# Attention and a two-layer mixer in one launch: when the third batch's q is loaded, and which queue turns it

## The chip, the cores and the metric

The kernel runs on one core of one Trainium2 chip. The metric is the device time of one execution in microseconds (us). The engines are named as in the profile: PE is TensorE (matmuls), PEld its weight loads, DVE is VectorE, ACT is ScalarE, POOL is GpSimd, SP is SyncE, which here only issues DMAs. A "q" behind an engine's name (SPq, ACTq) marks the DMA-issuing instructions of its queue. All transfers run on the core's 16 DMA engines, whoever issues them.

## The reference

All inputs are float32, and so is the output, of shape 8 × 384 × 1024.

```python
batch, n_q_heads, n_kv_heads, seq, head_dim = (8, 16, 4, 384, 64)
# attention: each of the 4 k/v heads serves 4 q heads
scores = scale * np.matmul(q, k.transpose(0, 1, 3, 2))
attn = softmax(scores)
x = np.matmul(attn, v)        # then heads side by side: (8, 384, 1024)
# mixer: over tokens, then over channels
tok = np.einsum('ts,bsd->btd', w_tok, alpha1 * x + beta1)
u = x + lam * tok
ch = np.maximum((alpha2 * u + beta2) @ w_ch1, 0.0) @ w_ch2    # 1024 -> 4096 -> 1024
out = u + lam * ch
```

## The kernel before

The work goes batch by batch, in eight **passes** (b = 0 to 7). A pass is what `main(b)` does: the two large products of batch b, with the attention and the token mixing of batch b + 1 (`side(b + 1)`) laid between its matmuls. Both matrices are bf16 on the chip.

**Phase 0 of a pass, "h"** (line 410): h = relu(a2 · W1). W1 (1024 × 4096) does not stay on the chip; it is read again in every pass, in 16 chunks of 256 columns (`load_w1`, 512 KB each as bf16), through a ring of five buffers (`RING`). GpSimd issues the load of chunk c + 5 as soon as chunk c's matmuls are done. Each chunk makes two 128-column tiles (`nt`) of 8 matmuls. ACT evacuates the even tiles and DVE the odd ones into `hT`. Two PSUM banks ("mm") take turns.

**Phase 1 of a pass, "ch"** (line 443): ch = h · W2, with W2 kept on the chip from the first pass on, in 2 × 3 output blocks of 32 matmuls each. Between every 4 matmuls there is room for a step of `side(b + 1)`: its scores (line 217, `scores3`), exp on ACT (line 226), attention times v (line 252), the token product (line 273) and a transposing DMA of the result into `a2T` (line 295), which is the next pass's h input.

**Slots.** `main` is a generator that yields 0 in phase 0 (twice per tile, 64 slots) and 1 in phase 1. The loop at the end of the kernel counts the yields of each phase and, at each count, calls what has been put down for that slot. The lists for `side` put the first `scores3` into slot 0 of phase 1. The list `moves` puts down loads and flips.

**q and k.** `load_k` reads k in float32 into `kst` (SP's queue), and `place_k` casts it into `k2` on GpSimd. `load_q` reads 16 heads of q in four loads of 4 heads each, with a cast to bf16, into the one buffer `q_raw` (GpSimd's queue, 192 KB each). `load_next(b)` does `place_k`, `load_q` and `load_v` in that order. The scores need q and k with the head dimension on partitions. For batches 0 and 1 PE transposes them. From batch 2 on a transposing DMA does: `flip_k` fills `kT` in one instruction, and `flip_q` fills `qT` in four, each for 4 heads (two of the eight pairs p). For batches 3 to 7 they are put into phase 1 of pass b − 2, at slots 34 to 43, on SP's queue, while that pass still works on the batch before; the scores of batch b follow in phase 1 of pass b − 1.

Batch 2 is the exception, since its loads come out of the busy start. Before the change its k and q are loaded at the end of phase 0 of pass 0, behind the first five W1 chunks of pass 1; the loads then wait their turn in GpSimd's DMA queue behind W2 and W1. They are flipped in phase 0 of pass 1, at slots 46 (k), 50, 54, 58 and 62 (q), from **ACT's** queue.

The order of instructions on every engine is the order in which the code records them (`manual_schedule`). Waits between engines are semaphores that the framework places. Each flip of q waits for the one load that fills its 4 heads.

Of the kernel before, what the change touches and what calls it, by code (L numbers as in the profile page):

```python
# [12 lines left out]
def kernel(  # L13
# [21 lines left out]
    nc = tc.nc  # L35
# [17 lines left out]
    NP = Hq // 2  # L53
    D1 = D + 1
    CW = 2
    NCH = NNT // CW
    RING = 5
# [21 lines left out]
    kT = const.tile([P, NST, Hkv, P], bf, tag="kT", name="kT")  # L79


    qT = const.tile([P, NP, NST, P], bf, tag="qT", name="qT")
# [3 lines left out]
    def by_st(ap):  # L86
        return ap.rearrange("h (p st) d -> p st h d", st=NST)
# [10 lines left out]
    def place_k(b, i, hs=(0, 1)):  # L98
        if b not in k2s:
            k2s[b] = sb.tile([P, NST, Hkv, 2, D], bf, tag="k2", name="k2", bufs=1)  # L100
        copies = [nc.gpsimd.tensor_copy] * 2
        if b == 1 or b == 0 == i:
            copies = (nc.vector.tensor_copy, nc.vector.tensor_copy if i else nc.scalar.copy)
        lo, hi = hs[0], hs[-1] + 1
        for a in range(2):
            copies[a](out=k2s[b][:, :, 2 * i + lo:2 * i + hi, a, :], in_=ks[b][i][:, lo:hi].rearrange("p h st d -> p st h d"))

    def load_v(b, sts=range(NST)):
        for st in sts:
            nc.gpsimd.dma_start(out=vt[b % 2][:, st, :, :D], in_=by_st(v[b])[:, st])  # L110

    def load_q(b):
        qrs[b] = sb.tile([P, Hq, NST, D], bf, tag="q_raw", name="q_raw", bufs=1)
        for h in range(0, Hq, G):
            nc.gpsimd.dma_start(out=qrs[b][:, h:h + G], in_=q[b, h:h + G].rearrange("h (p st) d -> p h st d", st=NST))

    def flip_queue(b):
        return nc.scalar if b == 2 else nc.sync

    def flip_k(b):  # L120
        flip_queue(b).dma_start_transpose(out=kT.rearrange("p st h s -> p (st h) s"),
                                    in_=k2s[b].rearrange("p st h a d -> p (st h a d)"))

    def flip_q(b, i=0, n=NP):
        flip_queue(b).dma_start_transpose(out=qT[:, i:i + n].rearrange("p a j s -> p (a j) s"),
                                    in_=qrs[b][:, 2 * i:2 * (i + n)].rearrange("p h st d -> p (h st d)"))

    w1src = moe_w_ch1.rearrange("(dt di) nf -> di dt nf", di=P)
# [3 lines left out]
    def load_w1(n):  # L132
        if n < B * NCH:
            t = sb.tile([P, NDT, CW * P], bf, tag="w1", name="w1", bufs=RING)
            c = n % NCH
            nc.gpsimd.dma_start(out=t, in_=w1src[:, :, c * CW * P:(c + 1) * CW * P])  # L136
            w1_tiles[n] = t

    def load_w2(dw, i, n):
        r, cs = slice(i * NNT // n, (i + 1) * NNT // n), slice(dw * 512, (dw + 1) * 512)  # L140
        nc.gpsimd.dma_start(out=w2[:, r, cs], in_=w2src[:, r, cs])

    def bank(shape, tag, name, dtype=f32):
        if tag == "mm":
            return mms.tile(shape, dtype, tag="mm", name=name, bufs=2)
        return psum.tile(shape, dtype, tag=tag, name=name, bufs=2 if tag == "sc" else 1)
# [9 lines left out]
    def evac(eng):  # L156
        return nc.scalar.copy if eng == "ACT" else nc.vector.tensor_copy
# [234 lines left out]
    def load_next(b):  # L392
        place_k(b, 0)
        place_k(b, 1)
        load_q(b)
        load_v(b)


    def main(b):
        a2T = a2Ts[b % 2]  # L400
        x = xs.pop(b)
        n = S + 1 if b == 0 else S
        for c in range(NCH):
            w1 = w1_tiles.pop(b * NCH + c)
            for j in range(CW):
                nt = c * CW + j
                begun = b == 0 and nt in early
                ps = early[nt] if begun else bank([P, 512], "mm", "h")
                for dt in range(0 if begun else NDT):
                    nc.tensor.matmul(out=ps[:, :n], lhsT=w1[:, dt, j * P:(j + 1) * P],  # L410
                                     rhs=a2T[:, dt, :n], start=(dt == 0), stop=(dt == NDT - 1))
                    if dt == 3:
                        yield 0
                c1 = bias1[:, nt:nt + 1]
                if b == 0:
                    evac("DVE" if nt % 2 else "ACT")(out=c1, in_=ps[:, S:n])
                if nt % 2 == 0:
                    nc.scalar.activation(out=hT[:, nt, :], in_=ps[:, :S], func=RELU, bias=c1)  # L418
                else:
                    nc.vector.tensor_scalar(out=hT[:, nt, :], in0=ps[:, :S], scalar1=c1,  # L420
                                            scalar2=0.0, op0=ADD, op1=mybir.AluOpType.max)
                yield 0

            if b or c + RING < NCH:
                load_w1(b * NCH + c + RING)
            if b == 0 and c == NCH - RING:
                for i in range(3, 8):
                    load_w2(0, i, 8)
                for i in range(8):
                    load_w2(1, i, 8)  # L430
            if b == 0 and c == NCH - 1:
                for i in range(RING):
                    load_w1(NCH + i)
                load_next(2)
        for dw in range(NDW):
            cs = slice(dw * 512, (dw + 1) * 512)
            for ms in range(NST):
                ps = bank([P, 512], "mm", "ch")
                o = sb.tile([P, 512], f32, tag="tmp", name="o", bufs=4)
                last = (b, dw, ms) == (B - 1, NDW - 1, NST - 1)  # L440
                for lo, hi in ((0, 256), (256, 384), (384, 512)) if last else ((0, 512),):
                    for nt in range(NNT):
                        nc.tensor.matmul(out=ps[:, lo:hi], lhsT=hT[:, nt, ms * P:(ms + 1) * P],  # L443
                                         rhs=w2[:, nt, dw * 512 + lo:dw * 512 + hi], start=(nt == 0), stop=(nt == NNT - 1))
                        if nt % 4 == 3 and nt < NNT - 1:
                            yield 1
                    c = slice(dw * 512 + lo, dw * 512 + hi)
                    nc.vector.tensor_tensor(out=o[:, lo:hi], in0=ps[:, lo:hi], in1=lam_t[:, c], op=MUL)  # L448
                    nc.vector.tensor_tensor(out=o[:, lo:hi], in0=o[:, lo:hi], in1=x[:, ms, c], op=ADD)  # L449
                    nc.sync.dma_start(out=out[b].rearrange("(p st) d -> p st d", st=NST)[:, ms, c], in_=o[:, lo:hi])  # L450
                yield 1
# [3 lines left out]
    with tc.manual_schedule(engines=order):  # L455
# [103 lines left out]
        for b in range(B):  # L559
            us = side(b + 1) if b + 1 < B else ({}, {})  # L560


            moves = []
            if b == 1:
                moves = [(0, 46 + 4 * i, flip_q, 2, 2 * i - 2, 2) if i else (0, 46, flip_k, 2) for i in range(5)]
            if 0 < b < B - 2:
                moves += [(1, 1, load_k, b + 2), (1, 2, load_next, b + 2), (1, 34, flip_k, b + 2), (1, 36, flip_q, b + 2, 0, 2),
                          (1, 37, flip_q, b + 2, 2, 2), (1, 42, flip_q, b + 2, 4, 2), (1, 43, flip_q, b + 2, 6, 2)]
            for i, u, *m in moves:
                us[i].setdefault(u, []).append(m)  # L570
            done = [0, 0]
            for second in main(b):
                if b == second - done[1] - 1 == 0:
                    lead_banks.close()
                    threes.append(ST(tc.psum_pool(name="threes", bufs=3)))
                for f, *a in us[second].get(done[second], []):
                    f(*a)
                done[second] += 1
# [28 lines left out]
```

The softmax here doesn't subtract the row's maximum and nothing guards it: scores larger than these inputs give would overflow.

## Time and profile before

| | |
|---|---|
| time, median of 3 | 806.16 us (805.33 to 807.13) |
| profiled span | 803.5 us |
| PE busy | 793.8 us (99%), 6123 matmuls |
| ACT busy | 226.9 us (28%) |
| DVE busy | 343.5 us (43%) |
| POOL busy | 178.5 us (22%) |
| moved by DMA | 113.17 MB, mean 141 GB/s |

A busy share tells how full an engine is over the whole span; where the kernel waits is read from the stages. The second pass, which the change touches, runs from 133.44 us (its first h matmul) to 232.50 us (the next pass's first). Its phase 1 begins at 176.75 us. In the profile's groups, `w` is a chunk of W1 or a part of W2, `sc` a bank of scores, `es` their exp, and `a<-b` reads "a is written from b". In the timeline a line gives start, duration, engine, source line, instruction, and in brackets how long the engine was idle before it and who ended that.

### The profile page before, as it was taken

The numbers are of one execution on the slowest core, as the hardware profiler recorded it, in microseconds if no ns is written. First come the engines' busy times: TensorE is split into PE (matmuls) and PEld (weight loads), VectorE is DVE, ScalarE is ACT, GpSimd is POOL, SyncE is SP. The second block draws the span as 40 slices with busy tenths as digits, with TensorE's granted clock in tenths as the row PEclk, the third lists the DMA queues.
The fourth block names the chain that finished last, engine by engine and source line by source line (L and its number), as shares of the span: only waits on it lengthen the run. The fifth ranks groups of instructions, "written<-read, shape, count | busy, mean of one in ns | idle before, by whom it ended". The sixth has DMA issues, their size and how long they took to land.

```text
span 803.5 us, 14220 instructions
## 1 busy us (share of the span) xinstructions
PE 793.8 (99%) x6123; PEld 452.0 (56%) x6123; DVE 343.5 (43%) x669; ACT 226.9 (28%) x309; POOL 178.5 (22%) x233
## 2 busy tenths in 40 slices
PE   8999999999999999999999999999999999999997
PEld 4766555655556555565555655566555655556545
DVE  8652465215552266322662236622366225552122
ACT  6624431223402233123221233122431223312100
POOL 7234231332013500135002340033400330003000
PEclk9999999999999999999999999999999999999999
DMA  9999999999269972999439991499914995129611
GB/s 190 202 186 202 205 207 170 187 186 170 66 126 188 198 101 58 162 189 196 74 73 169 193 196 43 92 174 197 163 46 114 165 198 88 48 61 187 82 40 40
DMA packets 234975, 113.17 MB, mean 141 GB/s; under 512 B 84376, under 2 KB 228768, under 8 KB 234912
## 3 DMA queue, kind: packets, MB, share of 16 engines
q0 software_dynamic: 170752, 83.47, 79.1%
q1 hardware_dynamic: 58848, 27.22, 13.5%
q10 hardware_dynamic: 5312, 1.57, 1.5%
q8 instruction: 48, 0.79, 0.4%
q14 instruction: 15, 0.12, 0.0%
HBM read 170.53 MB, written 12.58 MB: 228 GB/s over the span
## 4 chain that ended last, share of the span: by engine, by line
PE 84%; DMA 10%; issue 3%; DVE 1%; POOL 1%; ACT 0%; POOLq 0%
PE ch L443 37%; PE h L410 34%; DMA w<-in_moe_w_ch_dram 8%; PE sc L217 4%; PE sc L252 3%; PE sc L273 3%; DMA qT<-q_raw 1%; POOL w L136 1%; PE h L168 1%; PE tok L273 1%; PE av L252 0%; PE warm L460 0%; PE ut L290 0%; PE tp L203 0%; ACT hT L226 0%
## 5 line engine op out<-in xcount | busy, mean ns | idle before, releaser
L443 PE MATMUL ch<-w,hT 128*128 128x512 bf16 (+2 forms) x1600 | 357.7, 371 | 1.1 <-DVE o L448 0.9
L410 PE MATMUL h<-a2T,w 128*128 128x384 bf16 (+1 forms) x2016 | 331.5, 326 | 0.8 <-ACT hT L418 0.8
L410 PEld LDWEIGHTS <-w 128*128 128x128 bf16 x2016 | 196.8, 98 | 131.2 <-issue 1.5
L443 PEld LDWEIGHTS <-hT 128*128 128x128 bf16 x1600 | 144.6, 98 | 153.1 <-issue 10.5
L136 POOL DMA_DIRECT2D w<-in_moe_w_ch_dram x128 | 112.1, 878 | 519.3 <-PE h L410 500.5
L226 ACT ACTIVATE es<-sc 128x1024 bf16<-128x1024 f32 x126 | 121.4, 1023 | 187.9 <-PE sc L217 175.8
L420 DVE TENSOR_SCALAR hT<-h,bias 128x384 bf16<-128x384 f32 x128 | 79.1, 618 | 218.3 <-PE h L410 217.7
L418 ACT ACTIVATE hT<-h,bias 128x384 bf16<-128x384 f32 x128 | 74.3, 580 | 304.9 <-PE h L410 299.4
L448 DVE TENSOR_TENSOR o<-ch,vecs 128x512 f32<-128x512 f32 (+2 forms) x50 | 33.4, 669 | 107.8 <-PE ch L443 107.8
L252 PEld LDWEIGHTS <-es 128*128 128x128 bf16 x1008 | 38.2, 97 | 13.2
L273 PEld LDWEIGHTS <-wtokT 128*128 128x128 bf16 x576 | 37.3, 98 | 13.8 <-DVE x L258 1.7
L217 PE MATMUL sc<-qT,kT 64*128 64x384 bf16 (+2 forms) x576 | 41.9, 272 | 0.7 <-DMA qT<-q_raw 0.6
L257 DVE RECIPROCAL rinv<-sc 128x6 f32<-128x6 f32 x56 | 10.8, 193 | 68.4 <-PE sc L252 67.5
L252 PE MATMUL sc<-v,es 128*128 128x65 bf16 x1008 | 39.9, 193 | 0.0
L280 DVE TENSOR_TENSOR x<-sc,x 128x384 f32<-128x384 f32 x56 | 31.0, 553 | 20.0 <-PE sc L273 20.0
L273 PE MATMUL sc<-a,wtokT 128*128 128x128 bf16 x504 | 37.3, 219 | 0.0
L217 PEld LDWEIGHTS <-kT 64*128 64x128 bf16 x576 | 21.6, 94 | 24.5 <-issue 18.2
L449 DVE TENSOR_TENSOR o<-o,x 128x512 f32<-128x512 f32 (+2 forms) x50 | 33.5, 670 | 1.7
L284 DVE TENSOR_TENSOR a<-x,vecs 128x384 bf16<-128x384 f32 x56 | 32.7, 584 | 1.9
L265 DVE TENSOR_TENSOR a1f<-x,vecs 128x384 f32<-128x384 f32 x56 | 31.2, 558 | 1.9
L267 DVE TENSOR_TENSOR a<-a1f,vecs 128x384 bf16<-128x384 f32 x56 | 31.2, 558 | 1.9
L258 DVE TENSOR_TENSOR x<-sc,rinv 128x384 f32<-128x384 f32 x56 | 31.2, 558 | 1.9
(75 smaller groups left out, 203.1 us busy)
## 6 DMA issues: line engine op xcount, KB each, us to landing
w<-in_moe_w_ch_dram POOLq DMA_DIRECT2D x144, 512.0 KB, 8.6
out_dram<-o SPq DMA_DIRECT2D x47, 256.0 KB, 2.0
q_raw<-in_q_dram POOLq DMA_DIRECT2D x28, 192.0 KB, 8.1
kst<-in_k_dram SPq DMA_DIRECT2D x16, 192.0 KB, 3.4
v<-in_v_dram POOLq DMA_DIRECT2D x24, 64.0 KB, 7.9
a2T<-a SPq DMA_TRANSPOSE x56, 2.3
qg<-in_q_dram POOLq DMA_DIRECT2D x3, 192.0 KB, 5.9
stage<-in_q_dram ACTq DMA_DIRECT2D x2, 192.0 KB, 3.7
```

What stands on the lines that cost most here:

```text
L136: nc.gpsimd.dma_start(out=t, in_=w1src[:, :, c * CW * P:(c + 1) * CW * P])
L217: nc.tensor.matmul(out=sc[:, hh, k % 4:k % 4 + n], lhsT=kT[r, sk, 2 * p // G, :], rhs=qT[r, p, st:st + n, :], start=True, stop=True)
L226: nc.scalar.activation(out=e, in_=sc, func=EXP, scale=scale_qk)
L252: nc.tensor.matmul(out=av[:, hh, sq, :], lhsT=ess[k // 4][:, m % 2, k % 4, :], rhs=vb[:, sk, hk, :], start=(sk == 0), stop=(sk == NST - 1))
L273: nc.tensor.matmul(out=ps[:, tt, :], lhsT=wtokT[:, st, tt * P:(tt + 1) * P], rhs=a1s[p][:, st, :], start=(st == 0), stop=(st == NST - 1 an ...
L284: nc.vector.tensor_tensor(out=a2s[p], in0=u, in1=bc(al2, p), op=MUL)
L410: nc.tensor.matmul(out=ps[:, :n], lhsT=w1[:, dt, j * P:(j + 1) * P], rhs=a2T[:, dt, :n], start=(dt == 0), stop=(dt == NDT - 1))
L418: nc.scalar.activation(out=hT[:, nt, :], in_=ps[:, :S], func=RELU, bias=c1)
L420: nc.vector.tensor_scalar(out=hT[:, nt, :], in0=ps[:, :S], scalar1=c1, scalar2=0.0, op0=ADD, op1=mybir.AluOpType.max)
L443: nc.tensor.matmul(out=ps[:, lo:hi], lhsT=hT[:, nt, ms * P:(ms + 1) * P], rhs=w2[:, nt, dw * 512 + lo:dw * 512 + hi], start=(nt == 0), sto ...
L448: nc.vector.tensor_tensor(out=o[:, lo:hi], in0=ps[:, lo:hi], in1=lam_t[:, c], op=MUL)
L449: nc.vector.tensor_tensor(out=o[:, lo:hi], in0=o[:, lo:hi], in1=x[:, ms, c], op=ADD)
```

## The change

Three things are moved, all for batch 2; no arithmetic is added or removed.

1. Batch 2's q is no longer loaded at the end of pass 0. `place_k` and `load_v` stay there. `load_q(2)` now follows, on GpSimd's queue, the load of W1's last chunk for pass 1 (recorded when chunk 10 of pass 1 is done), ahead of the first five W1 chunks of pass 2.
2. Batch 2's k is flipped at slot 1 of phase 0 of pass 1, the head of that pass, instead of slot 46.
3. Its four q flips are all recorded at slot 46. All five flips go to SP's queue, like those of the later batches; ACT issues none any more.

On SP's queue the five flips now stand between the last output of pass 0 and the two `kst` loads for batch 3, which stood there before. The intention is to take the issuing of flips off ACT, which evacuates h in the same phase, and to take the q load out of the crowded first pass.

```diff
-    def flip_queue(b):
-        return nc.scalar if b == 2 else nc.sync
-
     def flip_k(b):
-        flip_queue(b).dma_start_transpose(out=kT.rearrange("p st h s -> p (st h) s"),
+        nc.sync.dma_start_transpose(out=kT.rearrange("p st h s -> p (st h) s"),
                                     in_=k2s[b].rearrange("p st h a d -> p (st h a d)"))

     def flip_q(b, i=0, n=NP):
-        flip_queue(b).dma_start_transpose(out=qT[:, i:i + n].rearrange("p a j s -> p (a j) s"),
+        nc.sync.dma_start_transpose(out=qT[:, i:i + n].rearrange("p a j s -> p (a j) s"),
                                     in_=qrs[b][:, 2 * i:2 * (i + n)].rearrange("p h st d -> p (h st d)"))
...
             if b == 0 and c == NCH - 1:
                 for i in range(RING):
                     load_w1(NCH + i)
-                load_next(2)
+                place_k(2, 0)
+                place_k(2, 1)
+                load_v(2)
+            if b == 1 and c == NCH - RING - 1:
+                load_q(2)
...
             if b == 1:
-                moves = [(0, 46 + 4 * i, flip_q, 2, 2 * i - 2, 2) if i else (0, 46, flip_k, 2) for i in range(5)]
+                moves = [(0, 1, flip_k, 2)] + [(0, 46, flip_q, 2, i, 2) for i in range(0, NP, 2)]
```

## The prediction, made before the changed kernel had run

> **What bounds the kernel now.** I read the page first, then the chain of waits in order of time, then the timeline of each engine around the changed stage, and last the landings of single transfers. The page's busy times and chain:
>
> ```profile
> PE 793.8 (99%) x6123; PEld 452.0 (56%) x6123; DVE 343.5 (43%) x669; ACT 226.9 (28%) x309; POOL 178.5 (22%) x233
> ...
> PE 84%; DMA 10%; issue 3%; DVE 1%; POOL 1%; ACT 0%; POOLq 0%
> ```
>
> TensorE (PE) is busy 99% of the span, so an edit that adds and removes no matmul can only win back a stall of PE. The change touches the second pass (b = 1), which begins at 133.44 us. PE's timeline there:
>
> ```profile
> 133.44 33.96 PE L410 MATMUL h<-a2T,w 128*128 128x384 bf16 x208
> 167.60 2.76 PE L410 MATMUL h<-a2T,w 128*128 128x384 bf16 x16 [0.19 <-ACT hT L418]
> 170.59 2.76 PE L410 MATMUL h<-a2T,w 128*128 128x384 bf16 x16 [0.23 <-ACT hT L418]
> 173.77 2.76 PE L410 MATMUL h<-a2T,w 128*128 128x384 bf16 x16 [0.41 <-ACT hT L418]
> 176.75 1.02 PE L443 MATMUL ch<-w,hT 128*128 128x512 bf16 x4 [0.23 <-ACT hT L418]
> 178.42 0.83 PE L217 MATMUL sc<-qT,kT 64*128 64x384 bf16 x12 [0.64 <-DMA qT<-q_raw]
> ...
> 232.50 41.76 PE L410 MATMUL h<-a2T,w 128*128 128x384 bf16 x256
> 274.11 1.03 PE L443 MATMUL ch<-w,hT 128*128 128x512 bf16 x4
> 275.06 0.83 PE L217 MATMUL sc<-qT,kT 64*128 64x384 bf16 x12
> ```
>
> The third pass is the ruler: its h stage runs from 232.50 to 274.11 = 41.6 us, and scores begin 0.95 us later. In the second pass h takes 176.75 − 133.44 = 43.3 us (1.7 too long) and scores begin 1.67 us later (0.7 too long). So 2.4 us is lost here, 0.30% of 806.16, in two ways. ScalarE (ACT) shows the first, and the landing of the first q flip the second:
>
> ```profile
> 163.78 3.14 ACTq L121 DMA_TRANSPOSE kT<-k  x1
> 166.97 0.58 ACT L418 ACTIVATE hT<-h,bias 128x384 bf16<-128x384 f32 x1 [2.85 <-PE h L410]
> 166.99 2.92 ACTq L125 DMA_TRANSPOSE qT<-q_raw  x1
> 169.96 0.58 ACT L418 ACTIVATE hT<-h,bias 128x384 bf16<-128x384 f32 x1 [2.41 <-PE h L410]
> ```
> ```profile
> 166.99 11.29 DMA qT<-q_raw
> 178.29 0.14 issue
> 178.42 0.83 PE sc L217 x12
> ```
>
> ACT issues each flip in about 3 us and cannot evacuate h meanwhile: its ReLUs, 2.60 us apart until then, slip to 3 us apart, and PE waits for the bank. The flip then lands at 166.99 + 11.29 = 178.28, and the first scores start 0.14 later.
>
> The other fact is that the DMA engines are full: 156 to 163 us shows 197 GB/s, so a W1 chunk (512 KB = 524 kB) takes 2.66 us, while PE eats one in 2.60. Single landings, in order: W1 issued at 159.9; W1 issued at 162.5; the third batch's first q load, issued at 103.80; a flip of `a2T`, issued at 103.50, under load, and one issued at 200.11 on idle engines:
>
> ```profile
> w<-in_moe_w_ch_dram POOLq DMA_DIRECT2D x1, 512.0 KB, 7.9
> ...
> w<-in_moe_w_ch_dram POOLq DMA_DIRECT2D x1, 512.0 KB, 9.4
> ...
> q_raw<-in_q_dram POOLq DMA_DIRECT2D x1, 192.0 KB, 23.5
> ...
> a2T<-a SPq DMA_TRANSPOSE x1, 6.8
> ...
> a2T<-a SPq DMA_TRANSPOSE x1, 2.3
> ```
>
> **What the Trainium skill says.** "DMA: Bandwidth & Descriptors", section "Issuing engines are not separate DMA queues": transfers from SP, ACT and GpSimd run on the same 16 engines and interleave; another issuer saves only issue time. The trace agrees: the flips on ACT landed after 11.3 us beside W1, and on SyncE (SP) after 2.8 in the later passes, where little else runs. The same page, "Queues, rings and completion order": each engine takes a ring's descriptors in order and round-robins between rings. So q loads queued behind W1 move after it, and flips share with it. The trace agrees: W1 issued at 100.77 landed at 126.55, and q, issued next, at 127.3, 128.3, 129.6 and 131.0. "TensorE: Matmul & The Clock Gate", "Part 1: The HAM clock gate": PE drops to half clock after an idle window of about 3.4 us. Here PE waits at most 0.64 us in this stage with the clock at 1.00, so no run shows it yet.
>
> **The change, part by part.**
>
> 1. ACT issues no flips. Removes the five 3 us blocks: h returns to 41.6 us, worth 1.7 us. PE then reaches the first scores at 133.44 + 41.6 + 0.95 = 176.0.
>
> 2. The k flip goes to SP at slot 1. SP's last output of the first pass is issued at 135.09, so the flip goes at about 135.5. Its data were cast at about 103, and the scores that read the old `kT` ended at 118. The engines are idle there: the flip on SP at 217.94 had its blocks through from 219.1 to 221.1 in the packet records, so here it moves at 136.7 to 138.7, and the pass's first W1 packets come at 138.2. The `kst` loads that ran in that gap go behind the q flips instead. Cost nothing: W1 lands 7.9 us after issue, and has 9.9 (issued 136.5, needed at 133.44 + 5 × 2.6 = 146.4).
>
> 3. The four q loads leave the end of the first pass, where PE has no stall: no gain. They are issued on GpSimd after W1 chunk 31 (162.5), at 163.4 to 165.6. The next pass's first five W1 chunks follow 1.3 us later; they are needed at 232: nothing.
>
> 4. When does q arrive? W1 chunk 31 landed at 162.5 + 9.4 = 171.9, with the k flip sharing the engines from 167.8 on. With the 7.9–8.0 of its forerunner it lands at 170.5. In the old place the first q load landed 0.75 us after the W1 before it: 171.3. Bounds: 170.9 (0.4 for the data alone) to 172.5 (W1 keeps its 9.4 and q adds 0.6).
>
> 5. The four q flips are recorded at slot 46 (164 us), but the first waits on SP for the first q load only, the next for the second, and so on. Queued behind them on SP are the two `kst` loads and the next output (188.3): nobody is in a hurry. The first flip is issued at 171.4. Cost under load: in the packet records, six flips issued while loads were queued saw their first block after 3.9 to 4.15 us (SP at 90.3, 101.0, 109.0, 115.3, 124.3, and ACT at 163.8; the one at 124.3 met q loads), against 1.2 on idle engines. Then 768 blocks: the ACT flips land 178.28 − 175.1 = 3.2 us apart beside W1. So 4.0 + 3.2 + 0.1 = 7.3 us, landing at 178.7. Bounds: 6.0 (blocks at twice that rate) to 8.9 (two `a2T` flips, 768 blocks in all, took 4.9 us beside W2). No bound goes to 2.8, since three q loads and the next W1 chunks are queued behind.
>
> 6. PE: first scores at 178.8 instead of 178.42, a wait of 2.8 us after 4 ch matmuls with nothing of PE's to hide it. The second flip lands 3.2 later, at 182, and its scores come some 15 us after the first: hidden.
>
> Sum: −1.7 (ACT) − 0.7 (old q wait) + 2.8 (new q wait) = +0.4 us, so 806.16 + 0.4 = 806.6.
>
> **Rivals.**
>
> A. The flips are hidden: all 2.4 us come back, 803.7 us. For it: flips on SP cost 2.8 us in every later pass, and then 171.3 + 0.1 + 2.8 = 174.2 is before 176.0. Against it: those ran on nearly idle engines; here W1 for the next pass follows directly. A half of it, with a flip of 4.6 to 5.4 us, gives a gain of over 1.6 us.
>
> B. Q comes later and the flip is slow: 172.5 + 0.1 + 8.9 = 181.5, a wait of 5.5 us, +3.1, so 809.3; if PE then also sits out a whole idle window of the clock gate, half speed for 3.4 us costs another 1.7: 811. For it: q sits at the tail of a queue that loses 0.06 us a chunk. Against: each term at its worst.
>
> C. The early k flip starves W1 in the second pass: 2.0 us of blocks against a slack of 9.9 − 7.9 = 2.0 us. It would cost up to 1 us in h: 807.6. Against: the engines are idle from 134 to 136 us.
>
> **How the numbers follow.** The forecast, one wait in place of another and ending within 1.6 us (0.2%) of before, 0.55: its terms vary by about 0.5 us each. C, mostly inside the same band, is counted there and at its edge. Slower by over 1.6 us needs first scores after 180.0: either q at 172.5 or a flip of 8.6, or some of both with C: 0.30, of which B's full size is 0.1. Faster by over 1.6 us needs the first scores by 176.8, a flip of at most 5.4 us: A, 0.15. For 8 in 10 I leave out the last tenth of each side: from 804.3, between A and the forecast, to 809.3, B without the clock gate.
>
> **What would show it.** Right: no `DMA_TRANSPOSE` on ACT and ReLUs 2.60 us apart through the pass's h; h of 41.6 us; the k flip on SP near 135.5; the first q flip issued on SP near 171.4 and landing over 6 us later; PE's first scores of the pass near 178.8 with a wait of about 2.8 on `qT`, and every later pass as before. Wrong: a first q flip that lands in 3 to 5 us (A), W1 landings of over 9.9 us with PE waiting for `w` inside h (C), or a PE clock below 1.00 after the wait (B).

## The result and the profile after

| | median, us | against before, 95% interval |
|---|---|---|
| before | 806.17 | |
| the changed kernel | 810.93 | 1.0059 [1.004, 1.0079] |
| the changed kernel, measured again with the experiments | 811.16 | 1.0059 [1.0047, 1.0072] |

The change costs 4.8 us. The page's lines of the changed kernel that answer to those shown of before (the matmul records of this profile are incomplete; the 6123 weight loads, PEld, are as many as before):

```profile
PE 790.1 (98%) x6056; PEld 452.6 (56%) x6123; DVE 342.5 (42%) x669; ACT 226.9 (28%) x309; POOL 178.8 (22%) x233
...
PE 95%; DMA 2%; DVE 1%; issue 1%; ACT 0%; POOL 0%
```

The second pass on PE's timeline (start us, duration us, engine, line, instruction, idle before it):

```profile
133.61 41.89 PE L407 MATMUL h<-a2T,w 128*128 128x384 bf16 x256
175.34 1.03 PE L444 MATMUL ch<-w,hT 128*128 128x512 bf16 x3
181.66 1.47 PE L214 MATMUL sc<-qT,kT 64*128 64x384 bf16 x12 [5.29 <-DMA qT<-q_raw]
183.06 4.81 PE L444 MATMUL ch<-w,hT 128*128 128x512 bf16 x16
...
237.56 41.76 PE L407 MATMUL h<-a2T,w 128*128 128x384 bf16 x256
```

h is one unbroken row: the small waits behind ACT are gone. ACT's timeline agrees, its ReLUs are 2.60 us apart to the end:

```profile
169.04 0.58 ACT L415 ACTIVATE hT<-h,bias 128x384 bf16<-128x384 f32 x1 [2.02 <-PE h L407]
171.64 0.58 ACT L415 ACTIVATE hT<-h,bias 128x384 bf16<-128x384 f32 x1 [2.02 <-PE h L407]
174.24 0.58 ACT L415 ACTIVATE hT<-h,bias 128x384 bf16<-128x384 f32 x1 [2.02 <-PE h L407]
```

But the scores begin 181.66 − 133.61 = 48.05 us after the pass began, where the third pass of before needed 42.56; before the change it was 44.98. And then the matmuls are slow: the first group of 12 scores takes 1.47 us instead of 0.83. The chain of waits shows where q comes from, and the stages show the clock (the columns are the stage, the busy times of the five engines with their instructions, the granted TensorE clock, the DMA share and GB/s):

```profile
162.69 0.86 POOL w L133
163.55 9.90 DMA q_raw<-in_q_dram
173.45 0.02 issue
173.47 8.05 DMA qT<-q_raw
181.52 0.14 issue
181.66 1.47 PE sc L214 x12
```
```profile
176.00:178.60 2.60, 0.37 (x2) 0.00 (x0) 0.16 (x1) 0.00 (x0) 0.87 (x1) 1.00 1.40 190
178.60:185.50 6.90, 3.84 (x18) 1.66 (x19) 0.00 (x0) 2.85 (x3) 0.00 (x0) 0.51 1.35 183
185.50:190.00 4.50, 4.45 (x36) 2.21 (x35) 1.45 (x4) 0.00 (x0) 0.00 (x0) 1.00 1.62 168
```

The first q load lands 9.9 us after its issue, the first flip 8.05 us after that. The W1 chunk just ahead of q in GpSimd's queue, issued at 162.69, takes 9.7 us:

```profile
w<-in_moe_w_ch_dram POOLq DMA_DIRECT2D x1, 512.0 KB, 9.7
```

In the stages PE sits idle, and its clock falls to half, from 178.6 to 185.5 us, of which some 3.8 us are work.

The balance is best drawn over the whole second pass, from its first h matmul to that of the next pass. An undisturbed pass, the third of before, takes 96.65 us (232.50 to 329.15). Before: 232.50 − 133.44 = 99.06. After: 237.56 − 133.61 = 103.95, that is 4.9 more, the whole loss. Of the 7.3 us over an undisturbed pass, 48.05 − 42.56 = 5.5 is the wait for q, and the other 1.8 is the clock. In the repetition (e10) the scores begin 47.18 us after the pass began (a wait of 4.6), but the pass takes 103.93 again: the clock took 2.7 there.

```profile
134.46 41.76 PE L407 MATMUL h<-a2T,w 128*128 128x384 bf16 x256
181.64 1.47 PE L214 MATMUL sc<-qT,kT 64*128 64x384 bf16 x12 [4.56 <-DMA qT<-q_raw]
238.39 3.90 PE L407 MATMUL h<-a2T,w 128*128 128x384 bf16 x23
```

### The profile page after: what moved, and what is told of

Read it like the earlier page. It is cut to its first block, busy times and chain, and to the rows that moved or that the text cites. A ratio compares the mean times of both kernels' runs of the same rounds, so it can differ in the third digit from the quotient of the medians.

```text
span 808.6 us, 14151 instructions
## 1 busy us (share of the span) xinstructions
PE 790.1 (98%) x6056; PEld 452.6 (56%) x6123; DVE 342.5 (42%) x669; ACT 226.9 (28%) x309; POOL 178.8 (22%) x233
## 4 chain that ended last, share of the span: by engine, by line
PE 95%; DMA 2%; DVE 1%; issue 1%; ACT 0%; POOL 0%
PE ch L444 41%; PE h L407 39%; PE sc L214 5%; PE sc L249 4%; PE sc L270 4%; DMA q_raw<-in_q_dram 1%; DMA qT<-q_raw 1%; PE h L165 1%; PE tok L270 1%; PE av L249 0%; PE warm L461 0%; PE ut L287 0%; PE tp L200 0%; ACT hT L223 0%; DVE x L255 0%
## 5 line engine op out<-in xcount | busy, mean ns | idle before, releaser
L444 PE MATMUL ch<-w,hT 128*128 128x512 bf16 (+2 forms) x1533 | 347.2, 371 | 4.4 <-issue 1.1
L249 PE MATMUL sc<-v,es 128*128 128x65 bf16 x1008 | 39.8, 193 | 0.0
```

What stands on the lines that cost most here:

```text
L249: nc.tensor.matmul(out=av[:, hh, sq, :], lhsT=ess[k // 4][:, m % 2, k % 4, :], rhs=vb[:, sk, hk, :], start=(sk == 0), stop=(sk == NST - 1))
```

## The experiments

In the table, "scores" is the time from the pass's first h matmul to its first scores (42.56 undisturbed), "pass" that to the next pass's first h matmul (96.65 undisturbed), both from the one profiled run. The pass begins between 133.3 and 135.1 us in these profiles, so everything is counted from its start. The two profiles of the changed kernel have their scores 0.9 us apart, so a difference under 1 us in that column says little. The kernel before was run again beside each group, with medians of 806.17 to 806.37 us; each ratio is to those runs.

| | time, us | ratio to before | scores | pass |
|---|---|---|---|---|
| before | 806.17 | | 44.98 | 99.06 |
| changed | 810.93 | 1.0059 [1.004, 1.0079] | 48.05 | 103.95 |
| e1: k flip in pass 0 | 809.76 | 1.0039 [1.0026, 1.0051] | 46.69 | 103.28 |
| e2: q load back | 810.26 | 1.0048 [1.0036, 1.006] | 49.29 | 103.38 |
| e3: before, flips on SP | 809.95 | 1.0047 [1.0035, 1.0059] | 48.94 | 103.02 |
| e4: all flips in pass 0 | 805.94 | 0.9993 [0.9985, 1.0001] | 44.51 | 98.60 |
| e5: unread matmuls in the wait | 808.6 | 1.0031 [1.0023, 1.004] | 47.32 | 101.40 |
| e6: next W1 later | 804.69 | 0.9981 [0.9973, 0.999] | 42.74 | 96.83 |
| e7: flips split | 803.91 | 0.9972 [0.9961, 0.9983] | 42.56 | 96.65 |
| e8: flips held on SP | 804.09 | 0.9974 [0.9963, 0.9985] | 43.97 | 98.06 |
| e9: e1 with unread matmuls | 808.01 | 1.0021 [1.0012, 1.0031] | 47.04 | 101.13 |
| e10: changed, again | 811.16 | 1.0059 [1.0047, 1.0072] | 47.18 | 103.93 |

**What the clock costs (e5).** Unread matmuls fill the place where PE would stand idle.

```diff
+        def fill_pe(n):
+            t = three()
+            for _ in range(n):
+                nc.tensor.matmul(out=t[:, 0].rearrange("p k s -> p (k s)"), lhsT=wtokT[:, 0, :P], rhs=w2[:, 0, :512],
+                                 start=True, stop=True)
...
+            if b == 1:
+                us[1][0] = [(fill_pe, 22)] + us[1][0]
```

> The changed kernel with 22 matmuls of 512 columns, whose result nobody reads, laid on PE just ahead of the first scores of pass 1: 22 x 0.216 = 4.75 us of work in the place where PE stands idle for 5.3 us, waiting for the first q flip. Theory (of the loss in the changed kernel some 1.9 us is the TensorE clock, which drops to half after the idle stretch and works 3.8 us of matmuls at half speed): the clock stays at 1.00, the scores begin at the same time, and the time falls by 1.9 us from 810.9 to 809.0. Rival (the pace after the wait comes from something else, such as exp or the flips that follow): 810.9 as before, or more.

Measured: 808.6 us. The same stages of this kernel:

```profile
176.00:178.60 2.60, 2.60 (x14) 1.18 (x12) 0.62 (x1) 0.00 (x0) 0.88 (x1) 1.00 1.41 192
178.60:185.50 6.90, 6.90 (x41) 3.17 (x40) 0.00 (x0) 2.86 (x3) 0.00 (x0) 1.00 1.35 183
```

The clock column reads 1.00 throughout. The scores begin when the added matmuls end, near where they began in the changed kernel, and the time is 2.3 us less: the theory holds, at a little more than its 1.9. The wait itself (47.32 − 42.56 = 4.8 us) is still there; only the clock's part is gone.

**Why the flip takes 8 us (e6).** The first five W1 chunks of pass 2, which the changed kernel issues straight behind q, are issued after batch 3's q and v loads instead.

```diff
-            if b or c + RING < NCH:
+            if (b or c + RING < NCH) and not (b == 1 and c >= NCH - RING):
                 load_w1(b * NCH + c + RING)
...
+            if b == 1:
+                moves += [(1, 3, load_w1, 2 * NCH + i) for i in range(RING)]
```

> The changed kernel with the first five W1 chunks of pass 2 issued after batch 3's q and v loads (some 20 us later) instead of straight behind batch 2's q loads, so that the q flips meet only the last q loads. Theory (a q flip costs 8 us in the changed kernel because W1 is queued behind it on the same DMA engines): the first q load still lands some 10 us after issue, but the first flip lands within 3 to 6.5 us of its issue, PE waits 0.5 to 3 us, the clock stays near 1.00, and the time is 804.5 to 807. Rival (the flip takes its 8 us in any case): PE waits 5 us again, 810 to 811.

Measured: 804.69 us. The flips on SP's timeline, and PE's start of phase 1:

```profile
173.04 1.21 SPq L122 DMA_TRANSPOSE qT<-q_raw  x1
```
```profile
134.44 41.76 PE L407 MATMUL h<-a2T,w 128*128 128x384 bf16 x256
176.04 1.03 PE L444 MATMUL ch<-w,hT 128*128 128x512 bf16 x4
177.18 0.83 PE L214 MATMUL sc<-qT,kT 64*128 64x384 bf16 x12
```

The first flip is issued at 173.04. By the packet records its first block moves at 174.43, 1.4 us later (3.9 in the changed kernel), and its 768 blocks are through at 176.28, after 1.85 us (3.4 in the changed kernel). The scores run at 177.18, 0.2 us late: 4.0 us from issue to landing (3.4 for the second flip) instead of 8. Q itself landed 38.6 us after the pass began, against 39.8 in the changed kernel and 39.1 in its repetition, so it explains only 0.5 to 1.2 us. So 4 of the flip's 8 us come from the W1 chunks that stand in the queue beside it, and without them the change wins 1.5 us instead of losing 4.8. The theory holds.

**Does the k flip push q back (e1, e9)?** The k flip moves from the head of pass 1 into the idle stretch before it.

```diff
             if b == 1:
-                moves = [(0, 1, flip_k, 2)] + [(0, 46, flip_q, 2, i, 2) for i in range(0, NP, 2)]
+                moves = [(0, 46, flip_q, 2, i, 2) for i in range(0, NP, 2)]
+            if b == 0:
+                moves = [(1, 42, flip_k, 2)]
```

> The changed kernel with one edit: batch 2's k is flipped in phase 1 of pass 0 (slot 42), where the DMA engines are about to fall idle, instead of at the head of pass 1. Theory (the k flip at the head of the pass pushes the whole W1 stream back, and with it the q loads behind it): the pass's first W1 chunk lands some 6 us after issue instead of 7.5 and its last some 8 instead of 9.7, the first q load lands near 171.7 instead of 173.45, PE waits some 3.5 us for the first q flip instead of 5.3, and the time falls to 807.5 if the TensorE clock then stays at full speed, to 809.3 if it drops. Rival (the k flip costs nothing and W1 is slower for another reason, such as the q loads): landings and time as in the changed kernel, 810.9.

Measured: 809.76 us, with the clock dropping again in the profiled run. Of the six runs, one kept a mean clock of 1.000 and took 806.9 us; the other five had 0.993 to 0.998 and took 809.0 to 810.6. That fits e5, but the one run has no trace, so whether its wait was shorter as well is not known. In the profile the scores come 1.4 us sooner than in the first profile of the changed kernel, which looked like the theory; but the changed kernel's own repetition came 0.9 sooner too. So the question was put again with the unread matmuls of e5 (17 of them), which take the clock out of it.

> The k flip of batch 2 in phase 1 of pass 0, as in the first experiment, together with 17 unread matmuls of 512 columns (3.7 us) ahead of the first scores, which keep the TensorE clock up during the wait. Theory (the k flip at the head of pass 1 delays W1 and, behind it, q by about 1.3 us, which the first experiment's drop of the clock had hidden): against the changed kernel with such matmuls (808.6) the first scores begin 1.2 to 1.4 us sooner, counted from the start of the pass, and the time is 807.3. Rival (the k flip's place doesn't matter for q): 808.6 again.

Measured: 808.01 us, against 808.6 for e5; the intervals overlap. The time lies between the theory's 807.3 and the rival's 808.6. The scores come 0.3 us sooner than in e5, not 1.2 to 1.4. The single landings of W1 show what became of the delay. First e9, the pass's first and last chunk, then the repetition of the changed kernel (e10), its last:

```profile
w<-in_moe_w_ch_dram POOLq DMA_DIRECT2D x1, 512.0 KB, 5.9
...
w<-in_moe_w_ch_dram POOLq DMA_DIRECT2D x1, 512.0 KB, 8.9
```
```profile
w<-in_moe_w_ch_dram POOLq DMA_DIRECT2D x1, 512.0 KB, 9.0
```

Without the k flip at its head the pass's first chunk lands 5.9 us after issue instead of 7.7 (e10), but the last one lands after 8.9 against 9.0. In both the lag grows along the pass. But it doesn't end alike in all runs: the last chunk took 9.7, 9.0, 9.1 and 8.5 us with the k flip at the head (the changed kernel, e10, e5, e6), 8.5 and 8.9 without it (e1, e9), and its forerunner in the kernel before 7.9. So e1's theory, that some 1.3 us pass on to q, did not show, and a smaller part can't be told from the scatter. What the k flip costs in time, by the intervals of e5 and e9 between nothing and some 2 us, stays open.

> The changed kernel itself, unedited, for a narrower time beside the experiments. All theories: 810.9 us within 0.5 us, and a wait of 5 to 5.5 us for the first q flip with the clock at half speed for some 3.5 to 5 us of the work after it.

Measured: 811.16 us; the two profiles of the same kernel split their 7.3 us differently between the wait and the clock, as shown above. Its wait, 4.6 us, lies below the 5 to 5.5 expected.

**Q back in its place (e2), and the kernel before with nothing but SP's queue (e3).** e2's edit, then e3's:

```diff
-                load_v(2)
-            if b == 1 and c == NCH - RING - 1:
-                load_q(2)
+                load_q(2)
+                load_v(2)
```
```diff
     def flip_queue(b):
-        return nc.scalar if b == 2 else nc.sync
+        return nc.sync
```

> The changed kernel with its q load put back to the end of pass 0; the k flip stays at the head of pass 1 and the four q flips at slot 46 on SP. Theory (the loss is the late q load): q is there when the flips are due, the first flip is issued near 164 and lands near 172, PE does not wait for it and the clock stays at 1.00. The flips then share the engines with the last W1 chunks, which were landing 0.2 us before PE needed them, so PE may wait for w in h by up to 1.5 us: 803.7 to 805.2 us. Rival (flips on SP beside W1 are slow whatever the q load does): PE waits for qT at the head of phase 1 by over 2 us and the time is 806 or more.

> The kernel before with one edit: its five flips of batch 2 go to SP's queue, at the same slots 46 to 62, with q loaded where it was. Theory (the first q flip's landing sets the end, whoever issues it, since the k flip stands in front of it): h goes back to 41.6 us (1.7 less), but the first q flip still lands near 178, so PE waits some 2.2 us at the first scores instead of 0.7, and the time is 806.0, the same within 0.3 us. Rival (the 1.7 us of ACT's blocked evacuations are won in full): 804.5 us.

Measured: 810.26 and 809.95 us. Both expectations missed on both sides: there is no wait for qT, and still about 4 us are lost. SP's timeline of e3, and below it PE's:

```profile
136.53 1.47 SPq L121 DMA_TRANSPOSE kT<-k  x1
138.10 9.73 SPq L125 DMA_TRANSPOSE qT<-q_raw  x4
```
```profile
134.44 16.00 PE L410 MATMUL h<-a2T,w 128*128 128x384 bf16 x96
152.49 7.05 PE L410 MATMUL h<-a2T,w 128*128 128x384 bf16 x32 [2.04 <-DMA w<-in_moe_w_ch_dram]
160.16 10.73 PE L410 MATMUL h<-a2T,w 128*128 128x384 bf16 x64 [0.62 <-DMA w<-in_moe_w_ch_dram]
171.87 10.71 PE L410 MATMUL h<-a2T,w 128*128 128x384 bf16 x64 [0.97 <-DMA w<-in_moe_w_ch_dram]
182.42 1.03 PE L443 MATMUL ch<-w,hT 128*128 128x512 bf16 x4
```

The q flips, recorded at slots 50 to 62, run at 138 us, at the head of the pass. A slot only fixes the order on each engine. ACT has a ReLU to do before the slot and gets there at 163.8; SP has nothing before it, so it issues the flips as soon as their data are there. There they take the DMA engines from W1, whose chunks then land up to 14.9 us after issue, and PE waits for `w`: h takes 182.42 − 134.44 = 48.0 us.

PE's second row holds something else: 32 matmuls take 7.05 us, where an undisturbed h needs 41.76 / 8 = 5.2 for as many. The stages of e3, in the columns of above, have the clock:

```profile
150.40:152.50 2.10, 0.06 (x2) 0.02 (x2) 0.62 (x1) 0.00 (x0) 0.88 (x1) 1.00 1.36 184
152.50:154.00 1.50, 1.50 (x6) 0.75 (x7) 0.00 (x0) 0.00 (x0) 0.00 (x0) 0.64 1.34 182
154.00:155.50 1.50, 1.50 (x6) 0.76 (x5) 0.00 (x0) 0.58 (x1) 0.00 (x0) 0.50 1.35 193
155.50:157.00 1.50, 1.50 (x8) 0.72 (x7) 0.02 (x1) 0.00 (x0) 0.00 (x0) 0.73 1.30 223
```

After a wait of only 2.04 us (2.09 in e2) PE works at half clock for some 3.4 us. It is not what costs the 4 us: of the ten runs of e2 and e3, five have a mean clock of 0.998 and take 809.5 to 810.6 us, the five with 1.000 take 809.3 to 810.6.

Issuing from ACT was a timer, and the kernel before paid its 1.7 us for that. In the changed kernel the late q load is the timer.

**A timer on SP (e8).** To e2, which has q loaded early, a small DMA is added ahead of the q flips that must wait for ACT's h tile of that slot.

```diff
+        held = const.tile([P, 16], bf, tag="held", name="held")
...
+        def gate():
+            nc.sync.dma_start(out=held, in_=hT[:, 22, :16])
...
-                moves = [(0, 1, flip_k, 2)] + [(0, 46, flip_q, 2, i, 2) for i in range(0, NP, 2)]
+                moves = [(0, 1, flip_k, 2), (0, 46, gate)] + [(0, 46, flip_q, 2, i, 2) for i in range(0, NP, 2)]
```

> The experiment with q loaded at the end of pass 0 and all q flips recorded at slot 46 on SP, with one more instruction: a tiny DMA on SP ahead of the q flips, that reads the h tile which ACT writes at the same slot. It adds a copy of 128 x 16 values that nobody uses. Theory (SP had no wait that held the flips at slot 46, so they ran at the head of the pass and cut into W1's stream from there on): now the first q flip is issued near 165 us, W1 lands under 10 us until then, the flips land from 172 to 181, only the last W1 chunk comes late, by up to 1.5 us, and the time is 804 to 805.5. Rival (the place in the pass doesn't matter, five flips cost W1 the same anywhere): about 6 us of waits for w, 810.

Measured: 804.09 us. SP, then PE:

```profile
164.11 0.57 SPq L466 DMA_DIRECT2D held<-hT  x1
164.78 9.41 SPq L122 DMA_TRANSPOSE qT<-q_raw  x4
```
```profile
133.40 39.16 PE L407 MATMUL h<-a2T,w 128*128 128x384 bf16 x240
173.80 2.77 PE L407 MATMUL h<-a2T,w 128*128 128x384 bf16 x16 [1.23 <-DMA w<-in_moe_w_ch_dram]
```

One instruction on SP turns the 4 us lost in e2 into 2 us won. Only the last chunk is late, as the theory said, by 1.23 us.

**Flips before the pass (e4, e7).** In e4 q is loaded early and all five flips are recorded in phase 1 of pass 0 (slot 42). In e7 only k and the first q flip are there; the other three come in phase 1 of pass 1, behind outputs that hold SP. Q is loaded as in e2; the rest of e7's edit:

```diff
-            if b == 1:
-                moves = [(0, 1, flip_k, 2)] + [(0, 46, flip_q, 2, i, 2) for i in range(0, NP, 2)]
+            if b == 0:
+                moves = [(1, 42, flip_k, 2), (1, 42, flip_q, 2, 0, 2)]
+            if b == 1:
+                moves = [(1, 7, flip_q, 2, 2, 2), (1, 15, flip_q, 2, 4, 2), (1, 15, flip_q, 2, 6, 2)]
```

> The changed kernel with q loaded at the end of pass 0 as before, and all five flips recorded in phase 1 of pass 0 (slot 42) on SP, so that they move in the idle stretch of the DMA engines between 131 and 139 us. Theory (both kernels lose only by having flips or q loads in the W1 stream of pass 1): no wait for qT, h of 41.6 us, first scores at 176.0, the whole 2.4 us of the kernel before is won: 803.7 us. Rival (the 6 us of flips now push W1 of pass 1 back beyond its slack of some 2 us): PE waits for w in h and the time is 805 to 808.

> Q loaded at the end of pass 0 as in the kernel before; the k flip and only the first q flip (the heads of the first scores) recorded in phase 1 of pass 0 on SP, the other three q flips in phase 1 of pass 1 at slots 7 and 15, on SP behind outputs that hold them there. Theory (flips cost PE time only where they run in the W1 stream of pass 1's phase 0): half of the flips' blocks move in the idle stretch of the DMA engines before the pass and the rest after W1's ring is full; h is 41.6 us, there is no wait for qT, and the time is 803.8, 0.3% under the kernel before. Rival (the two early flips still push W1 beyond its slack, or the later flips come too late for their scores): PE waits for w in h, or for qT inside phase 1, and the time is 805 to 807.

Measured: 805.94 us for e4, which its interval can't tell from no change, and 803.91 for e7. In e4 there is no wait for qT, but W1 lands 10.1 to 11.0 us after issue from the second chunk on and PE waits for it, as the rival had it. In e7 nothing is left to wait for:

```profile
135.07 41.76 PE L407 MATMUL h<-a2T,w 128*128 128x384 bf16 x256
176.67 1.03 PE L443 MATMUL ch<-w,hT 128*128 128x512 bf16 x4
177.63 0.83 PE L214 MATMUL sc<-qT,kT 64*128 64x384 bf16 x12
```

W1 lands after at most 9.4 us there. The pass takes 96.65 us, as the third pass of before does, and the kernel is 0.28% under the kernel before, the lowest of all, with e8's interval overlapping.

## Why the prediction was wrong

The forecast was 806.6 us; measured were 810.93, past the end of the range (809.3). Three terms of the sum failed: when q arrives, how long the flip takes, and what PE's wait costs besides its own length. Rival B gave 809.3 without and 811 with the clock's drop, by the mechanism that came; it had a chance of 0.1. That its landing of the flip, 181.5, is also the measured one is in part luck: its q at 172.5 was 0.95 us too early, its flip of 8.9 us 0.85 too long.

1. ACT's blocks: right. h is one row of 41.9 us by the profile, and PE would have had its scores 42.7 us after the pass began.
2. The k flip at the head, costed at nothing: right for PE (h is 41.9 us against 41.76, so at most 0.1 us of waiting for `w`); for q not settled (e9 against e10). The first chunk was delayed by 1.8 us, which only rival C had in view.
3. The move of the q load out of the first pass: no gain to be seen, as said (the pass begins at 133.61 instead of 133.44).
4. **When q arrives: a mis-sized term.** Forecast 171.3, 7.9 us after its issue; measured 173.45, 9.9 after it (9.2 in e10). The step took the 7.9 of the forerunner for W1's last chunk, which landed after 9.7 us in the changed kernel (9.0 in e10). Why the stream was up to 1.8 us later than before is open; with the k flip out of the way it was still 8.5 and 8.9 (e1, e9). Q then landed 1.1 us behind that chunk, not 0.75. This the step could have had: its own figures, 192 KB (197 kB) at 197 GB/s, give 1.0 us for q's data, not the 0.4 and 0.6 of its bounds. Q came after the later bound, 172.5.
5. **The flip under load: a mis-sized term.** Forecast 4.0 + 3.2 + 0.1 = 7.3; measured 8.05. By the packet records the first block moved at 177.41, 3.9 us after issue, as forecast, and the 768 blocks were through at 180.81, 3.4 later. What was missing is the time from the last block to the landing: 0.7 us, where the step had 0.1. The 3.2 was the distance of two landings in a row, in which that time does not appear. The kernel before had it too: the last block of its k flip moved by 174.30, and the landing came at 175.08. That the load causes 4 of the 8 us is shown by e6. The mechanism of this step was right. (Its lower bound, with blocks at twice the rate, comes to 4.0 + 1.6 + 0.1 = 5.7 and not 6.0; nothing hangs on it.)
6. **The sum, where PE stands idle without further cost: a term put at nothing.** The Trainium skill, "TensorE: Matmul & The Clock Gate", "Part 1: The HAM clock gate", says that the clock halves after an idle window of about 3.4 us, and the forecast put the drop only into the worst case of B. The trace shows the drop: half clock from 178.6 to 185.5 in the changed kernel, and in e1 too after a wait of 4.1. But it doesn't agree with 3.4 us as a limit below which a wait is safe: in e3 and e2 the clock halved after waits of 2.04 and 2.09 us. Waits of up to 1.23 us (e8) were not followed by a drop. So the 2.8 us of the forecast were already long enough to put the clock at risk. e5 shows the price in the changed kernel, 2.3 us.

Together, from the start of the pass: q came 2.0 us later than forecast, the flip and the start of the scores took 0.7 more, and the clock took 1.8. With the forecast's +0.4 that is +4.9 us, what the pass lost. In e10 the three are 1.3, 0.55 and 2.7, the same sum within 0.1.

Rival C (W1 starves inside h) did not come; it came in e2, e3, e4 and e8, where flips ran in W1's stream. The bound used against it, 9.9 us from issue to need, held to about 0.1 us: PE waited for W1 in the kernels whose landings passed 10 us (up to 15.3, 14.9, 11.0 and 11.3 in e2, e3, e4 and e8) and by about 0.1 us at most in the others (10.0 at most in the changed kernel, 9.4 in e7).

## What to carry to other kernels

- Before moving a DMA to another queue, ask what held it at its place. A queue with no other work runs ahead to the first wait, so the old queue's compute may have been a timer; one small DMA that reads the right tile can take that part (e8).
- A short transfer that the critical path needs, issued into a stream that saturates the DMA engines, costs what stands beside it: here 8 us instead of 4 with only q loads beside it (e6) and 2.8 on nearly idle engines. Place it where the engines are idle, or put the bulk behind it (e6, e7).
- A wait on PE can cost more than its length: here waits of 4.1 to 5.5 us were followed by 6.8 us at half clock, and waits of 2.0 and 2.1 us by 3.4. A forecast that leaves PE idle for some 2 us or more should carry that cost in its likeliest case, not in its tail.

## What had not been expected of the hardware

The clock halved after waits of only 2.04 and 2.09 us (e3, e2), and stayed at half for some 3.4 us there and 6.8 us after the longer waits.

The 3 us for issuing a flip are not peculiar to ACT. In the kernel before, issuing a flip of the same size took ACT 2.9 us beside W1, and SP 1.24 us in a later pass on nearly idle engines. But in the changed kernel SP, beside W1, took 1.21, 1.67, 3.21 and 3.27 us for its four flips in a row: the issue became as slow there.

Seven flips that were issued with several loads queued beside them, on either queue, began to move 3.9 to 4.15 us after issue (six in the kernel before, and the changed kernel's first q flip), against 1.2 us on idle engines. Full DMA engines alone don't explain it: in e6, where only the last three q loads were left, the engines moved 191 GB/s, and the first block came after 1.4 us; in e2, with one W1 load just issued, after 3.1. What sets this time stays open.

Two runs of the same kernel had q landing 0.7 us apart and the wait for it 0.9 apart, and the same total.
